# A fused attention and token/channel mixer: the short tile's weight parts stacked, the last pair's products in another order, and other orders for the planner

## The chip, the cores and the metric

The kernel runs on one core of a Trainium2 chip. The metric is the device time of one execution in microseconds. Matmuls run on TensorE (PE; its weight loads appear as PEld), elementwise work on VectorE (DVE), ScalarE (ACT) and GpSimd (POOL). SyncE (SP) issues the DMA transfers in this kernel; they leave its queue in order.

## The reference

For 8 batches of 8 heads, 576 positions and width 64, two attentions are added: one on q, k and v averaged over groups of four positions (144 x 144 scores, the result repeated four times), and a local one with scores for |i - j| < 4. The result x (576 x 512 per batch) goes through a token MLP across the positions and a channel MLP:

```python
q_d = q.reshape(B, H, Sd, 4, D).mean(axis=3)     # also k_d, v_d
out_up = np.repeat(sm_attn(q_d, k_d, v_d), 4, axis=2)
scores = np.where(np.abs(pos[:, None] - pos[None, :]) < 4, scale * q @ k.T, -1e9)
x = out_up + softmax(scores) @ v
h = np.maximum(x.T @ w_tok1, 0) @ w_tok2         # 576 -> 256 -> 576
u = x + h.T
out = u + np.maximum(u @ w_ch1, 0) @ w_ch2       # 512 -> 1536 -> 512
```

## The kernel before

**Attention.** Per batch, `pool_q` and `load_v` sum q, k and v in groups of four (qd, vd; v arrives in eight pieces, vr). `pooled` works on four pairs of heads: scores sd (line 503), their row maximum mxd, the exponential pd, its transpose td (line 531), the product ad with vd (line 541), and the division into od (line 551). `pd` is made in two ways: in the batches of `BIASED` ACT takes the exponential with the negative maximum as bias, four instructions a pair (line 515); in the others DVE subtracts (line 521, two a pair) and ACT takes one exponential (line 524). `local` works on five tiles of positions (`TILES`; four of 128 rows, the last, short one of 64): scores sc, the masked softmax P (line 600 multiplies by the reciprocal sum r), its transpose pT, copied to pt, and the product av with vw (line 619). vw holds v for the local windows in its rows, loaded with line 466, and in further rows the pooled result od, written there by a DMA (line 557): so one av product gives the sum of both attentions. av has to wait for that write.

**Token MLP** (`mix`). t1 adds up, over the five tiles, x of a tile times the first token weight. In batch 0 x and W are plain float32 (line 672). From batch 1 on both are split in a high part and the remainder (xh, made by ACT, line 658, and DVE, line 660; W1[t] has the two parts side by side), and `mm3` multiplies three of the four combinations (`PASSES`: high by high, high by remainder, remainder by high). In the short tile only 64 of the 128 partitions hold data. t2 is the second token product; its result plus x is scaled and split as uh, in 16 bit.

**Channel MLP.** Batches 0 and 1 are computed plainly (c1 from uh and CW, c2 from h and CX). Batches 2 to 7 use a seven-product scheme on 2 x 2 blocks: `first_blocks` goes over six pairs n, each with the products B11, T1, T2, B22, B21, T3 and T4, collected in cx, cy and cz, and in the loop T3 and T4 of a pair stand among the products of the next pair; `after` makes the sums s, y, u and the inputs h of the second layer from them (s reads cz, y reads cx after T3, and T4 may only be added to cx when y has read it). `second_blocks` then makes 2 x 7 products dX, dY, dZ of 18 matmuls each, that is 3 for each of the six pairs.

**Order.** No engine's order is written by hand. Every piece of work is a generator that says with `step(engine, us, needs...)` what it would run next; `drive` (lines 172 to 212) keeps a clock per engine and takes the step that can start first. Among steps on one engine that start within `PATIENCE` of each other it takes the one whose generator stands first in the list; `PRIORITY` is the order of the groups in that list (p pooled, A local, W and w token weights, U the up part of batch 0, and so on). While batch 0's uh is not ready, `keep_busy` fills gaps on PE with matmuls of a constant tile ("busy<-junk"). SP's order follows from the same steps; a weight load also waits until the third load before it has landed (`in_turn`). In SP's order C1 to C2 names the channel weights (raw), W0 to W8 the token weights (raw).

Of the kernel before, what the change touches and what calls it, by code (L numbers as in the profile page):

```python
# [6 lines left out]
F32 = mybir.dt.float32  # L7
F32R = mybir.dt.float32r
F16 = mybir.dt.float16
# [26 lines left out]
DEPTH = 3  # L36
PRIORITY = "LpWUMASETaCDPHmQw"


@with_exitstack  # L40
def tile_ups_attention_mixer(ctx, tc, qk, vw, vr, w1, w2, c1, c2, out):
# [83 lines left out]

    def mm3(ps, lhs, rhs, first, last, **kw):
        for i, (a, c) in enumerate(PASSES):
            nc.tensor.matmul(ps, lhs(a), rhs(c), start=first and i == 0, stop=last and i == 2, **kw)  # L128

# [10 lines left out]

    clock = dict(A=2.0, G=5.0, V=2.0, P=0.0, S=0.0, D=0.0, R=0.0, X=0.0)
    now = [0.0]
# [29 lines left out]
    def drive(streams):  # L172
# [3 lines left out]
        while True:  # L176
# [37 lines left out]
    def to_f32(raw, at, y=None, *needs):  # L214

        n = raw.shape[1] // 2
        words = raw.rearrange("p (n two) -> p n two", two=2)
        lo, hi = words[:, :, 0], words[:, :, 1]
        yield step("A", 0.1 + n * 0.0011, at=at)
        nc.scalar.activation(hi.bitcast(F32), hi.bitcast(F32), AF.Prelu, scale=2.0 ** -112, alpha=-2.0 ** 32)  # L220
        yield step("G", 0.1 + n * 0.0016)

        nc.gpsimd.tensor_scalar(lo, lo, 2.0 ** -29, -0.501, ALU.mult, ALU.add)
        e = yield step("V", 0.08 + n * 0.0012, *needs, port=True)
        nc.vector.scalar_tensor_tensor(lo if y is None else y(), hi, 3, lo, ALU.logical_shift_left, ALU.bitwise_or)
        return e
# [48 lines left out]
    class Channel:  # L275
# [31 lines left out]
        def parts(self, i):  # L307
            y = self.place[i + 2]
            f = self.place[i].bitcast(F16).rearrange("p (a n) -> p a n", a=2)
            yield step("A", 0.72)  # L310
            nc.scalar.activation(f[:, 0], y, AF.Copy, scale=self.s[i // 4])
            t = yield step("V", 0.75, port=True)
# [102 lines left out]
    def load_v(st):  # L415
# [53 lines left out]
    def pool_q(st, hp):  # L469
# [92 lines left out]
    def local(st, t):  # L562
# [35 lines left out]
        nc.vector.reciprocal(r, r)  # L598
        yield step("V", 0.5, at=0.0, port=True)
        nc.vector.tensor_tensor(w, w, r.unsqueeze(2).unsqueeze(2).to_broadcast([n, H, 8, 5]), ALU.mult)  # L600
        before = [("av", b, t - 2)] if t > 1 else [("av", b - 1, 3 + t)] if b else []
# [42 lines left out]
    def mix(st):  # L644
# [8 lines left out]
        def splits():  # L653
            for t in range(NT if b else 0):
                yield step("A", 0.62, ("x", b, t), *([("over", 0, 0)] if b == 1 else []),
                           *([("t1", b, t - 3)] if t > 2 else [("mixed", b - 1)] if b > 1 else []))
                xh = st.xh[t] = T([128, 2, 512], F32R, "xh", f"xh{b}_{t}")
                nc.scalar.copy(xh[:, 0], xf(t))
                e = yield step("V", 0.7, port=True)
                nc.vector.tensor_tensor(xh[:, 1], xf(t), xh[:, 0].bitcast(F32), ALU.subtract)  # L660
                make(("xh", b, t), e)

        def products():
            for t in range(NT):
                e = yield step("P", 1.8 if b == 0 else 1.5 if b == 1 else 1.42, *([("W", "split", t), ("xh", b, t)] if b else [("W", "y", t), ("x", 0, t)]),
                               take="" if t else f"gg>{b}")
                if t == 0:
                    st.acc = P2(f"t1_{b}")
                for f in range(2):
# [342 lines left out]

    PER_BATCH = 12 + 2 * len(SECOND)
    blocks_ = {}

    def first_blocks(b):
# [13 lines left out]

        for n in range(NP + 1):
            m = n - 1
            if n < NP:
                p = blocks_[b, n] = Batch()
                e = yield go(n, 0, "B11", take=f"m>X{b}_{n}")
                p.h = T([128, 7, 2, HALF], F16, "h7", f"h{b}_{n}")
                H.append(p.h)
                p.a = unit[base + 2 * n]
                p.X = PM(f"cx{b}_{n}")[:, :HALF]
                product(p.X, p.a[:, 0], "B11", True)  # L1040
                make(("product", b, n, "B11"), e)
            if m >= 0:
                q = blocks_[b, m]
                e = yield go(m, 1, "T3", ("uc", b, m))
                product(q.X, q.b[:, 1], "T3", False)
                make(("product", b, m, "T3"), e)
            if n < NP:
                e = yield go(n, 0, "T1", take=f"m>Y{b}_{n}")
                p.Y = PM(f"cy{b}_{n}")[:, :HALF]
                product(p.Y, p.a[:, 1], "T1", True)  # L1050
                make(("product", b, n, "T1"), e)
            if n < NP:
                e = yield go(n, 0, "T2", ("s", b, n))
                product(p.X, p.a[:, 2], "T2", False)
                make(("product", b, n, "T2"), e)
            if m >= 0:
                e = yield go(m, 1, "T4", ("c22", b, m))
                product(q.X, q.b[:, 2], "T4", False)
                make(("product", b, m, "T4"), e)
                make(("used", base + 2 * m + 1), e)  # L1060
            if n < NP:
                e = yield go(n, 0, "B22", ("y", b, n))
                product(p.Y, p.a[:, 3], "B22", False)
                make(("product", b, n, "B22"), e)
                make(("used", base + 2 * n), e)
                e = yield go(n, 1, "B21", take=f"g>Z{b}_{n}")
                p.b = unit[base + 2 * n + 1]
                p.Z = P1(f"cz{b}_{n}")[:, :HALF]
                product(p.Z, p.b[:, 0], "B21", True)
                make(("product", b, n, "B21"), e)  # L1070
        make(("first", b), e)

    def after(b, n):
# [82 lines left out]
        def z_chain():  # L1156
# [6 lines left out]
            make(("got", "t4", b, n), e)  # L1163
            e = yield step("V", 0.46, give=f"m>X{k}")
            lo_relu("B21", p.X)
# [11 lines left out]
    def second_blocks(b):  # L1177
# [3 lines left out]

        def product(ps, w, x, first_):
            i = PARTS.index(x)
            for k in range(6):
                for j, (a, c) in enumerate(PASSES):
                    nc.tensor.matmul(ps, w[:, k, a], H[k][:, i, c], start=first_ and k == j == 0,  # L1186
                                     stop=k == 5 and j == 2, skip_group_check=True)

        for o in range(2):
            at = st.at = {}  # L1190
            for i, name in enumerate(SECOND):
# [3 lines left out]
                needs = [] if new else [("into", b, o, {"S2": "A11", "S3": "S2", "A22": "S3", "S4": "S1"}[name])]  # L1195
                e = yield step("P", 2.21, ("unit", k), *(("h", b, n, OF[name]) for n in range(len(FIRSTS))), *needs,
                               at=0.0, take="" if not new else f"m>{kind}{b}_{o}z")
                if new:
                    at[kind] = PM(f"d{kind}{b}_{o}")[:, :HALF]
                product(at[kind], unit.pop(k), OF[name], new)  # L1200
                blocks_[b, o, name] = at[kind]
# [181 lines left out]
```

## Time and profile before

| | us |
|---|---|
| median of 3 runs | 897.86 |
| lowest, highest | 896.86, 899.55 |
| the profiled execution | 899.88 |
| its span, first to last instruction | 897.9 |
| PE, DVE, ACT, POOL busy | 857.5, 634.4, 418.9, 395.1 |

The span leaves out 2.0 us of the profiled execution's time, before the first and after the last instruction. Its mean granted clock is 0.974 of full speed. In the rows below a timeline row has start, duration, engine, line, operation, "out<-in", shapes and a count; in brackets stands the idle time before it, and what ended it. A group's row has busy time and mean duration behind the bar, then idle time and its releasers. A wait's row has total, number and longest.

### The profile page before, as it was taken

What the parts mean: (1) busy time and instruction counts of PE and PEld (TensorE: products, weight loads), DVE (VectorE), ACT (ScalarE), POOL (GpSimd) and SP (SyncE); (2) the same over time, 40 slices, a digit from 0 to 9 for tenths busy, and PEclk for the clock granted to TensorE, in tenths of its full rate; (3) what the DMA queues carried; (4) which work ended last, traced back from release to release, by engine and by line L of the source; (5) the groups of instructions that cost most, each with busy time, mean ns of one, the idle gap of its engine ahead of it and who ended that gap; (6) DMA issues with size and microseconds to landing.
All of it is one profiled execution on the core that took longest, in us unless ns stands there. A gap on an engine that the chain in (4) does not pass through costs nothing.

```text
span 897.9 us, 26687 instructions
## 1 busy us (share of the span) xinstructions
PE 857.5 (95%) x11112; PEld 691.5 (77%) x11112; DVE 634.4 (71%) x1410; ACT 418.9 (47%) x978; POOL 395.1 (44%) x593
## 2 busy tenths in 40 slices
PE   8798999898999999999999999999999999999998
PEld 6666777686779877888778887878768786887776
DVE  6669999667886756858576876678576875656662
ACT  2366553134553335744375526654265525642640
POOL 6228475868596203662077404752067401420330
PEclk9589999898999999999999999999999999999999
DMA  7875523663364308645673466544664464237653
GB/s 243 283 263 192 164 63 118 233 209 93 95 222 118 92 27 291 218 127 158 197 275 121 134 199 230 200 139 156 223 233 137 130 196 124 95 112 214 203 161 122
DMA packets 71656, 152.85 MB, mean 170 GB/s; under 512 B 16560, under 2 KB 32432, under 8 KB 69488
## 3 DMA queue, kind: packets, MB, share of 16 engines
q1 hardware_dynamic: 71536, 151.16, 51.5%
q8 instruction: 87, 1.43, 0.6%
q14 instruction: 33, 0.27, 0.1%
HBM read 128.32 MB, written 20.45 MB: 166 GB/s over the span
## 4 chain that ended last, share of the span: by engine, by line
PE 81%; DVE 9%; DMA 4%; ACT 2%; POOL 2%; issue 2%; SPq 1%; ACTq 0%; DVEq 0%; POOLq 0%
PE dX L1186 12%; PE c L128 11%; PE t L128 11%; PE cx L1025 10%; PE dY L1186 6%; PE cy L1025 6%; PE ad L541 3%; PE cz L1025 3%; PE dZ L1186 3%; PE av L619 3%; PE sc L577 2%; PE pT L605 2%; PE td L531 2%; PE sd L503 2%; PE t L690 2%
## 5 line engine op out<-in xcount | busy, mean ns | idle before, releaser
L1098 POOL TENSOR_TENSOR h<-t,h 128x288 f16<-128x288 f32 x108 | 83.2, 772 | 213.6 <-ACT h L1087 212.6
L1025 PEld LDWEIGHTS <-wa 128*128 128x128 f16 x864 | 82.3, 98 | 27.1 <-issue 4.7
L1186 PEld LDWEIGHTS <-wc_S 128*128 128x128 f16 x864 | 83.4, 98 | 21.0 <-issue 0.2
L1025 PEld LDWEIGHTS <-wb 128*128 128x128 f16 x648 | 63.0, 99 | 20.1 <-issue 3.9
L128 PE MATMUL c<-h,CX 128*128 128x288 f16 x576 | 76.3, 289 | 0.6 <-DVE CX L313 0.5
L128 PE MATMUL c<-uh,CW 128*128 128x288 f16 x576 | 75.2, 286 | 0.4 <-issue 0.4
L1186 PEld LDWEIGHTS <-wc_A 128*128 128x128 f16 x648 | 62.9, 98 | 15.7 <-issue 0.2
L487 POOL TENSOR_TENSOR qd<-qk 128x144 f32<-128x144 f32 x48 | 30.9, 644 | 87.5 <-DMA qk<-in_qk_dram 87.5
L128 PEld LDWEIGHTS <-CX 128*128 128x128 f16 x576 | 55.6, 99 | 16.4 <-DVE CX L313 1.2
L128 PEld LDWEIGHTS <-CW 128*128 128x128 f16 x576 | 55.1, 98 | 14.3 <-issue 1.0
L1025 PE MATMUL cx<-uh_T,wb 128*128 128x288 f16 x432 | 64.9, 287 | 1.1 <-DVE y L1129 1.1
L457 POOL TENSOR_TENSOR vr<-vr 72x256 f32<-72x256 f32 x48 | 37.0, 770 | 60.3 <-DMA vr<-in_vr_dram 51.2
L128 PE MATMUL t<-xh,W 128*128 128x512 f32 x210 | 58.8, 414 | 4.7 <-DVE xh L660 2.5
L487 POOL TENSOR_TENSOR qd<-qd,qk 128x144 f32<-128x144 f32 x96 | 60.6, 631 | 6.3
L128 PE MATMUL t<-W,hid 128*128 128x288 f32 x336 | 58.4, 309 | 0.0
L1186 PE MATMUL dX<-h,wc_S 128*128 128x288 f16 x432 | 56.9, 286 | 0.0
L1186 PE MATMUL dY<-h,wc_S 128*128 128x288 f16 x432 | 56.9, 286 | 0.0
L1186 PE MATMUL dX<-h,wc_A 128*128 128x288 f16 x432 | 56.0, 286 | 0.0
L1087 ACT ACTIVATE h<-t 128x288 f16<-128x288 f32 x108 | 47.6, 442 | 12.6 <-DVE t L1102 12.5
L1227 DVE SCALAR_TENSOR_TENSOR u<-dX,io,u 128x288 f32<-128x288 f32 x48 | 24.8, 517 | 34.0 <-PE dX L1186 33.7
L128 PEld LDWEIGHTS t<-xh,W 128*128 128x128 f32 x210 | 37.1, 188 | 15.2 <-DVE xh L660 5.1
L128 PEld LDWEIGHTS t<-W,hid 128*128 128x128 f32 x336 | 46.6, 189 | 0.0
(206 smaller groups left out, 1957.5 us busy)
## 6 DMA issues: line engine op xcount, KB each, us to landing
qk<-in_qk_dram SPq DMA_DIRECT2D x32, 580.0 KB
wa<-d1a SPq DMA_DIRECT2D x36, 512.0 KB
wc_S<-d_S SPq DMA_DIRECT2D x48, 384.0 KB
wb<-d1b SPq DMA_DIRECT2D x36, 384.0 KB
wc_A<-d_A SPq DMA_DIRECT2D x36, 384.0 KB
vw<-in_vw_dram SPq DMA_DIRECT2D x8, 1280.0 KB
vr<-in_vr_dram SPq DMA_DIRECT2D x64, 144.0 KB
vw<-in_vw_dram SPq DMA_DIRECT2D x8, 1024.0 KB
```

Source lines behind the costliest of these rows:

```text
L128: nc.tensor.matmul(ps, lhs(a), rhs(c), start=first and i == 0, stop=last and i == 2, **kw)
L457: nc.gpsimd.tensor_add(t[:, 0:2], t[:, 0:2], t[:, 2:4])
L487: nc.gpsimd.tensor_add(to, to if f > 1 else x[0], x[f])
L503: nc.tensor.matmul(ps[:G, par, Sd * g:Sd * g + Sd], st.qd[p, pr, 0, G * g:G * g + G], st.qd[p, pr, 1], start=True, stop=True)
L531: nc.tensor.transpose(ps[:G, par, o:o + G], pd[:, par, g, G * kg:G * kg + G], ident[:G, :G])
L541: nc.tensor.matmul(ps[:, g, par], pt[:, par, kg, G * g:G * g + G], st.vd[:, kg, 2 * pr + par], start=kg == 0, stop=kg == 1)
L619: nc.tensor.matmul(ps[QB * j:QB * j + QB, par, D * hp:D * hp + D], pt[p, hp, QB * j:QB * j + QB], st.vw[p, g, h, D * hp:D * hp + D], start ...
L1025: nc.tensor.matmul(ps, w[:, a, 128 * k:128 * k + 128], uh[x][:, k, c], start=first_ and k == j == 0, stop=k == 1 and j == 2, skip_group_ch ...
L1087: nc.scalar.activation(here().h[:, PARTS.index(name), 0], x, f)
L1098: nc.gpsimd.tensor_tensor(h[:, i, 1], getattr(here(), x), h[:, i, 0], ALU.subtract)
L1186: nc.tensor.matmul(ps, w[:, k, a], H[k][:, i, c], start=first_ and k == j == 0, stop=k == 5 and j == 2, skip_group_check=True)
L1227: nc.vector.scalar_tensor_tensor(u, blocks_[b, o, name], io, u, ALU.mult, ALU.add)
```

## The change

- The short tile's two weight parts are stacked: the high part in partitions 0 to 63 and the remainder in 64 to 127 of one half of W1, the high part once more in the other half. xh of the short tile has the high part of x in both halves of the partitions (two copies by ACT). Two passes (`STACKED`) then cover the three combinations.
- In `first_blocks` the last pair's T3 stands ahead of its B21, and T4 behind it. In `second_blocks` the products of o = 0 are divided: 15 matmuls for the first five pairs, then 3 for the last, which alone need the last pair's h.
- vr of batch 0 lies in the eight buffers of u instead of those of x, xh and od.
- `BIASED` holds all batches; P times r runs on POOL in batch 0; batch 7's cx lies in the "gg" banks.
- `PATIENCE`, `PRIORITY`, the costs of several steps and the filler's size (at most 12 instead of 8, for 0.85 instead of 0.6 of a gap) are other numbers.

```diff
+STACKED = ((0, 0), (1, 1))
-PATIENCE = 0.15
+PATIENCE = 0.1
-BIASED = range(2, 8)
+BIASED = range(0, 8)
-PRIORITY = "LpWUMASETaCDPHmQw"
+PRIORITY = "pLSUMAWTaCEDPHmQw"
...
-                    keep_busy(min(8, int((t - clock["P"]) * 0.6 / 0.22)))
+                    keep_busy(min(12, int((t - clock["P"]) * 0.85 / 0.22)))
...
         nc.scalar.copy(f[:, 0], WY[i])
+        if f.shape[0] == short:
+            nc.scalar.copy(f[:, 1], WY[i])
...
-        nc.vector.tensor_tensor(f[:, 1], WY[i], f[:, 0].bitcast(F32), ALU.subtract)
+        nc.vector.tensor_tensor(W1[-1][short:, 0] if f.shape[0] == short else f[:, 1], WY[i], f[:, 0].bitcast(F32), ALU.subtract)
...
-            tag = "x" if st.b or i < 4 else "xh" if i < 7 else "od"
-            ts[i] = T([G, 4, 128], F32, tag, f"vr{st.b}_{i}")
+            ts[i] = T([G, 4, 128], F32, "x" if st.b else "u", f"vr{st.b}_{i}")
...
-        nc.vector.tensor_tensor(w, w, r.unsqueeze(2).unsqueeze(2).to_broadcast([n, H, 8, 5]), ALU.mult)
+        (nc.gpsimd if b < 1 else nc.vector).tensor_tensor(w, w, r.unsqueeze(2).unsqueeze(2).to_broadcast([n, H, 8, 5]), ALU.mult)
...
-                nc.scalar.copy(xh[:, 0], xf(t))
+                if t < NT - 1:
+                    nc.scalar.copy(xh[:, 0], xf(t))
+                else:
+                    for p in (0, short):
+                        nc.scalar.copy(xh[p:p + short, 0], xf(t)[:short])
...
-                            t == 0, t == NT - 1)
+                            t == 0, t == NT - 1, PASSES if t < NT - 1 else STACKED)
...
+            if n == NP - 1:
+                yield from third(n)
+            e = yield go(n, 1, "B21", take=f"g>Z{b}_{n}")
+            p.b = unit[base + 2 * n + 1]
+            p.Z = P1(f"cz{b}_{n}")[:, :HALF]
+            product(p.Z, p.b[:, 0], "B21", True)
+            make(("product", b, n, "B21"), e)
+        e = yield from fourth(NP - 1)
...
+                early = NP - 1 if o == 0 else NP
...
+                product(at[kind], w, OF[name], new, range(early))
+                if early < NP:
+                    e = yield step("P", 2.21 / NP, ("h", b, early, OF[name]), at=0.0)
+                    product(at[kind], w, OF[name], False, range(early, NP))
```

Three places show how the orders differ. The first is SP's queue in the opening, where od0's write to vw0 is issued. Before:

```order
L241 DMA C15_raw_495<-in_c1_dram 128x1024
L241 DMA W5_raw_602<-in_w2_dram 128x576
L241 DMA W6_raw_627<-in_w2_dram 128x576
L241 DMA W7_raw_692<-in_w2_dram 128x576
L241 DMA W8_raw_706<-in_w2_dram 128x576
L557 DMA vw0_338<-od0_452 8x9x512 x2
L241 DMA C16_raw_892<-in_c1_dram 128x1024
```

and now:

```order
L242 DMA C15_raw_589<-in_c1_dram 128x1024
L242 DMA W5_raw_775<-in_w2_dram 128x576
L559 DMA vw0_412<-od0_425 8x9x512 x2
L242 DMA W6_raw_793<-in_w2_dram 128x576
L242 DMA W7_raw_799<-in_w2_dram 128x576
L242 DMA W8_raw_871<-in_w2_dram 128x576
L242 DMA C16_raw_915<-in_c1_dram 128x1024
```

The write has moved past the loads of W6, W7 and W8.

The second is PE's order where batch 2's pooled attention begins (the first number in a name is the batch, the second of sd, td and ad the pair of heads; c1_1_0_0 is a plain product of batch 1). Before:

```order
L503 MATMUL sd2_0_3158<-qd2_2411 72x144 x4
L503 MATMUL sd2_1_3169<-qd2_2411 72x144 x4
L531 MATMUL td2_0_3190<-ident_67,pd2_0_3179 72x72 x8
L531 MATMUL td2_1_3209<-ident_67,pd2_1_3200 72x72 x8
L541 MATMUL ad2_0_3233<-vd2_2819,ptd2_0_3221 72x65 x8
```

and now, where sd2_0 and sd2_1 stand directly ahead of c1_1_0_0's twelve matmuls, of which the first row is the last:

```order
L129 MATMUL c1_1_0_0_3265<-uh1_0_3_3241,CW0_140 128x288
L637 MATMUL um1_1_t_3290<-ident_67,um1_1_m_3281 1x128
L533 MATMUL td2_0_3293<-ident_67,pd2_0_3257 72x72 x8
L643 MATMUL um1_1_b_3305<-um1_1_m1_3292,ones_72 128x1
L533 MATMUL td2_1_3312<-ident_67,pd2_1_3283 72x72 x8
L129 LDWEIGHTS CW1_141
```

A whole product of batch 1 has come in between sd and td, and ad2_0 has moved behind a further one.

The third is DVE's order at the end of batch 7's last pair (number 5), before:

```order
L1091 SCALAR_TENSOR_TENSOR h7_4_13135<-cx7_4_13136,h7_4_13135 128x288
L1111 TENSOR_TENSOR s7_5_13234<-cz7_5_13279,s7_5_13234 128x288
L1151 TENSOR_TENSOR u7_5_13264<-cy7_5_13238,u7_5_13264 128x288
L1129 TENSOR_TENSOR y7_5_13253<-cx7_5_13217,y7_5_13253 128x288
L1102 SCALAR_TENSOR_TENSOR t17_5_13315<-s7_5_13234,u7_5_13264 128x288
```

and now:

```order
L1168 TENSOR_TENSOR u7_5_13336<-cy7_5_13310,u7_5_13336 128x288
L1108 SCALAR_TENSOR_TENSOR h7_4_13209<-cx7_4_13210,h7_4_13209 128x288
L1128 TENSOR_TENSOR s7_5_13306<-cz7_5_13364,s7_5_13306 128x288
L1146 TENSOR_TENSOR y7_5_13327<-cx7_5_13291,y7_5_13327 128x288
L1119 SCALAR_TENSOR_TENSOR t17_5_13387<-s7_5_13306,u7_5_13336 128x288
```

u has moved ahead of s; y stands behind s in both, while on PE the product that s reads (B21) now comes after the one that y reads (T3).

Over the program the order has 9702 rows on PE instead of 9574; among them 216 junk matmuls instead of 152 and 196 products t<-xh,W instead of 210.

More of the change, by code (lines that the diff above doesn't have):

```diff
@@ L124, in tile_ups_attention_mixer, with mm3 @@
         nc.vector.tensor_copy(p[:, :, 3:53:7], rep.unsqueeze(1).to_broadcast([128, H, QB // 4]))
-    def mm3(ps, lhs, rhs, first, last, **kw):
-        for i, (a, c) in enumerate(PASSES):
-            nc.tensor.matmul(ps, lhs(a), rhs(c), start=first and i == 0, stop=last and i == 2, **kw)
+    def mm3(ps, lhs, rhs, first, last, passes=PASSES, **kw):
+        for i, (a, c) in enumerate(passes):
+            nc.tensor.matmul(ps, lhs(a), rhs(c), start=first and i == 0, stop=last and i == len(passes) - 1, **kw)
     def pow2(src, f, inv, s, least=2.0 ** -60):
@@ L134, in pow2 @@
         nc.vector.reciprocal(s, inv)
[L141 removed]
+    clock = dict(A=2.0, G=5.0, V=2.0, P=0.0, S=0.0, D=1.5, R=0.0, X=0.0)
     now = [0.0]
@@ L1013, in tile_ups_attention_mixer, with X_IN @@
     PER_BATCH = 12 + 2 * len(SECOND)
+    def X_IN(b):
+        return "gg" if b == B - 1 else "m"
     blocks_ = {}
@@ L1029, in go @@
             return step("P", 0.74, ("unit", base + 2 * n + u), ("uh", b, x), *needs, at=0.0, take=take)
[L1031 to L1070, printed above, removed]
@@ new lines, in third, with fourth @@
+        def third(m):
+            q = blocks_[b, m]
+            q.b = unit[base + 2 * m + 1]
+            e = yield go(m, 1, "T3", ("uc", b, m))
+            product(q.X, q.b[:, 1], "T3", False)
+            make(("product", b, m, "T3"), e)
+        def fourth(m):
+            q = blocks_[b, m]
+            e = yield go(m, 1, "T4", ("c22", b, m))
+            product(q.X, q.b[:, 2], "T4", False)
+            make(("product", b, m, "T4"), e)
+            make(("used", base + 2 * m + 1), e)
+            return e
@@ new lines, in first_blocks @@
+        for n in range(NP):
+            p = blocks_[b, n] = Batch()
+            e = yield go(n, 0, "B11", take=f"{X_IN(b)}>X{b}_{n}")
+            p.h = T([128, 7, 2, HALF], F16, "h7", f"h{b}_{n}")
+            H.append(p.h)
+            p.a = unit[base + 2 * n]
+            p.X = (PM(f"cx{b}_{n}") if X_IN(b) == "m" else P2(f"cx{b}_{n}")[:, 0])[:, :HALF]
+            product(p.X, p.a[:, 0], "B11", True)
+            make(("product", b, n, "B11"), e)
+            if n:
+                yield from third(n - 1)
+            e = yield go(n, 0, "T1", take=f"m>Y{b}_{n}")
+            p.Y = PM(f"cy{b}_{n}")[:, :HALF]
+            product(p.Y, p.a[:, 1], "T1", True)
+            make(("product", b, n, "T1"), e)
+            e = yield go(n, 0, "T2", ("s", b, n))
+            product(p.X, p.a[:, 2], "T2", False)
+            make(("product", b, n, "T2"), e)
+            if n:
+                yield from fourth(n - 1)
+            e = yield go(n, 0, "B22", ("y", b, n))
+            product(p.Y, p.a[:, 3], "B22", False)
+            make(("product", b, n, "B22"), e)
+            make(("used", base + 2 * n), e)
+            if n == NP - 1:
[5 more added lines that the diff above has]
+            make(("product", b, n, "B21"), e)
@@ L1180, in second_blocks, with product @@
         H, base = st.H, PER_BATCH * (b - 2) + 12
-        def product(ps, w, x, first_):
+        def product(ps, w, x, first_, ks):
             i = PARTS.index(x)
-            for k in range(6):
+            for k in ks:
                 for j, (a, c) in enumerate(PASSES):
@@ L1195, in second_blocks @@
                 needs = [] if new else [("into", b, o, {"S2": "A11", "S3": "S2", "A22": "S3", "S4": "S1"}[name])]
-                e = yield step("P", 2.21, ("unit", k), *(("h", b, n, OF[name]) for n in range(len(FIRSTS))), *needs,
+                NP = len(FIRSTS)
+                early = NP - 1 if o == 0 else NP
+                e = yield step("P", 2.21 * early / NP, ("unit", k), *(("h", b, n, OF[name]) for n in range(early)), *needs,
                                at=0.0, take="" if not new else f"m>{kind}{b}_{o}z")
```

20 lines of the change are left out of this document (10 added, 10 removed).

## The prediction

> **What bounds the kernel now.** I read the page first, then the list of waits by engine, then windows by stage, then the timeline of the places that stood out.
>
> ```profile
> span 897.9 us, 26687 instructions
> PE 857.5 (95%) x11112; PEld 691.5 (77%) x11112; DVE 634.4 (71%) x1410; ACT 418.9 (47%) x978; POOL 395.1 (44%) x593
> ```
>
> TensorE is busy 857.5 of 897.9 us, the next engine 71% of them: TensorE is the bound. There are three ways to gain: fewer matmuls, fewer of the 40.4 idle us, and fewer matmuls at a low clock. The windows (PE busy, then the other engines, then PEclk in the third column from the right) say where idle and low clock lie:
>
> ```profile
> 0.00:85.00 85.00, 72.92 (x1034) 56.71 (x1035) 60.59 (x142) 41.27 (x82) 41.18 (x78) 0.84 0.70 239
> 131.00:250.00 119.00, 107.59 (x1653) 87.50 (x1652) 89.89 (x197) 46.02 (x101) 78.83 (x112) 0.94 0.46 151
> 345.00:898.00 553.00, 538.32 (x6645) 435.14 (x6633) 377.08 (x843) 270.12 (x661) 205.89 (x307) 1.00 0.54 174
> ```
>
> The first 85 us lose 12.1 us to idling and run at 0.84, 131 to 250 lose 11.4 at 0.94, the long rest from 345 on loses 14.7 out of 553. So the opening and the stage of batch 1 hold most of what an order of work can win. PE's waits over the run:
>
> ```profile
> PE av L619 <- DMA vw<-od: 7.6, 5, 3.1
> PE td L531 <- ACT pd L515: 7.5, 5, 3.2
> PE t L128 <- DVE xh L660: 2.5, 3, 1.8
> PE t L128 <- ACT xh L658: 2.0, 2, 1.2
> ```
>
> **A: the write of od0 leaves SP earlier.** SP's timeline and the chain of waits:
>
> ```profile
> 20.07 12.45 SPq L241 DMA_DIRECT2D C_raw<-in_c_dram  x6
> 33.56 5.58 SPq L241 DMA_DIRECT2D W_raw<-in_w_dram  x4
> 39.19 1.56 SPq L557 DMA_DIRECT2D vw<-od  x2
> 40.06 4.16 DMA vw<-od
> 35.41 0.42 DVE L551 TENSOR_TENSOR od<-ad,rd 72x256 f32<-72x256 f32 x1
> 46.23 5.48 PE L672 MATMUL t<-x,W_y 128*128 128x512 f32 x8
> 55.33 3.70 PE L672 MATMUL t<-x,W_y 128*128 128x512 f32 x8
> ```
>
> od0 is finished at 35.83, but its write stands behind four W loads, issued from 33.56 to 39.14. It is issued at 39.19, lands at 44.22, and the av matmuls wait for it. Afterwards it stands behind the first W load only, at about 33.9. For that od0 must be done by then: before, the od buffer waited for POOL's last read of vr0_7; now v lies in other buffers and the pd subtractions are off DVE. With the same 5.0 us from issue to landing, av starts 39.2 - 33.9 = 5.3 us earlier. The eight t matmuls after it cost 5.48 us against 3.70 warm: another 1.8 if the shorter idling keeps the clock. If od0 were no earlier than 35.83, the write could go then: -3.4. The far end is 0, if the loads under way hold its landing where it is. I take **-5.3**, since both issue times are in rows. The POOL multiply by r replaces one on DVE ahead of pT; POOL waited for loads in these microseconds, so I cost it at nothing; if it queues behind a conversion there, the price is about that of DVE's part of one, 0.62 in the rows below.
>
> **B: the first c products.** Per group on DVE or PE:
>
> ```profile
> L521 DVE TENSOR_TENSOR pd<-sd,mxd 72x288 f32<-72x288 f32 x16 | 6.5, 448 | 0.3
> L600 DVE TENSOR_TENSOR P<-P,r 128x320 f32<-128x320 f32 (+1 forms) x40 | 21.2, 530 | 0.7
> L510 DVE TENSOR_SCALAR mxd<-mxd 72x4 f32<-72x4 f32 x24 | 6.4, 267 | 0.8
> L515 ACT ACTIVATE pd<-sd,mxd 72x144 f32<-72x144 f32 x96 | 28.3, 373 | 26.2 <-DVE mxd L510 14.2 <-PE ad L541 10.9 <-issue 1.1
> L524 ACT ACTIVATE pd<-pd 72x576 f32<-72x576 f32 x8 | 5.5, 682 | 19.7 <-DVE pd L521 19.6
> 47.72 2.48 DVE L225 SCALAR_TENSOR_TENSOR CW<-C_raw 128x512 uint32<-128x512 uint32 x4
> 72.07 1.14 DVE L225 SCALAR_TENSOR_TENSOR CW<-C_raw 128x512 uint32<-128x512 uint32 x1
> 82.33 2.04 PE L170 MATMUL busy<-junk 128*128 128x192 bf16 x13
> 84.54 1.65 PE L128 MATMUL c<-uh,CW 128*128 128x288 f16 x12
> 92.88 8.98 PE L128 MATMUL c<-uh,CW 128*128 128x288 f16 x72
> ```
>
> Ahead of the first c's input DVE loses 8 pd (8 x 0.448 = 3.6) and 5 products by r (5 x 0.53 = 2.7), and gains 5 CW conversions (5 x 0.62 = 3.1) and 4 mxd multiplies (4 x 0.267 = 1.1): net 2.1 less. On PE, 13 junk matmuls (2.04) fill the time until c, and from 84.54 to 92.88 four groups of 1.65 take 8.34 us, a loss of 1.7. So 3.7 can go at most, nothing at least. I take **-2.1**, DVE's saving, because DVE holds that stretch. The five conversions then no longer sit between c products. The softmax of a pair in batches 0 and 1 was a chain of two pd on DVE and one exp on ACT, 2 x 0.448 + 0.682 = 1.58; now it is four exps on ACT, 4 x 0.373 = 1.49. On the path that is even; ACT works 0.81 more per pair, 3.2 per batch, which its idle half (41.27 of 85 us busy) covers; uncovered it would eat the 2.1.
>
> A price that speaks against this part: one CW conversion took 0.62 us with POOL idle (first of the two CW rows) and 1.14 at 72 us, with POOL at work. The Trainium skill, SBUF — State Buffer, "Who interferes with whom", says that a VectorE instruction with two SBUF inputs contends with a GpSimd instruction that reads SBUF; these two rows agree. By that rule the five multiplies now on POOL could each lengthen a conversion by 0.5, 2.6 in all, and B would come out at +0.5.
>
> **C: batch 1's start, 131 to 250.**
>
> ```profile
> 168.42 1.46 SPq L557 DMA_DIRECT2D vw<-od  x2
> 171.81 0.27 PE L619 MATMUL av<-vw,pt 64*32 64x64 f32 x2 [2.44 <-DMA vw<-od]
> 176.06 3.08 PE L128 MATMUL c<-h,CX 128*128 128x288 f16 x12
> 212.64 0.69 PE L531 MATMUL td<-ident,pd 72*72 72x72 f32 x8 [3.21 <-ACT pd L515]
> 214.14 1.18 PE L531 MATMUL td<-ident,pd 72*72 72x72 f32 x8 [0.80 <-ACT pd L515]
> 215.00:220.00 5.00, 5.00 (x156) 4.41 (x154) 2.96 (x9) 0.98 (x3) 4.47 (x9) 0.50 0.21 57
> ```
>
> Before, td of batch 2 stood right behind sd and waited 3.21 + 0.80 = 4.0 us; now c products of batch 1, independent of the softmax, stand between: -4.0, nothing late behind them but td itself, which has 12 products (1.65 us) and more of cover. The clock was 0.50 behind this gap, and low behind the 2.4 us wait for vw1 too: the c row at 176 takes 3.08, where the same twelve took 1.65 at 84.54. Half clock cost about 1.5 there and 2.5 behind td (half of the five us from 215). I take 2.0 of these 4.0, the share of the td gap, and leave the 3.7 us of av waits in this window as they are. Bounds: 0, if new waits take their place, and -15 (11.4 idle plus 4 of clock). I take **-6.0**.
>
> The Trainium skill, TensorE: Matmul & The Clock Gate, "Part 1: The HAM clock gate", has the array fall to half rate after an idle window of about 3.4 us and return after as much busy time. The 3.21 gap with 0.50 behind it agrees nearly; a 2.44 gap was enough at 171.81, so the measured one decides. By the rule alone the 216 junk matmuls (152 before) would keep the opening warm too, and A would be -7.1.
>
> **D: batches 2 to 7.** The waits there are those of 345 to 898, and the end of batch 7's last pair:
>
> ```profile
> PE td L531 <- ACT pd L515: 3.5, 3, 1.2
> 861.91 0.45 DVE L1129 TENSOR_TENSOR y<-cx,y 128x288 f32<-128x288 f32 x1
> 862.42 0.90 PE L1025 MATMUL cx<-uh_T,wb 128*128 128x288 f16 x6 [0.55 <-DVE y L1129]
> ```
>
> In batches 2 to 5 the first 15 matmuls of a second step now run between sd and td: they hide the 3.5. In batches 6 and 7 nothing is left to put there, and T4 waits for y as before. But y stands behind s on DVE, and s reads B21's sum, which PE now computes after T3. B21 ends where T3 did, 861.87 by the row of T4 less its wait; s and y, of 0.45 each, then end near 862.8: T4 is 0.4 later, twice, +0.8 (0 if DVE catches up). Together **-2.7**, bounds +0.8 and -5.7 (the xh waits of 2.5 and 2.0 gone as well, the tail at nothing).
>
> **E: the short tile.**
>
> ```profile
> 258.98 1.39 PE t L128 x6
> L128 PE MATMUL t<-xh,W 128*128 128x512 f32 x210 | 58.8, 414 | 4.7 <-DVE xh L660 2.5 <-ACT xh L658 2.0
> L658 ACT CAST xh<-x_last 128x512 fp32r<-128x512 f32 x7 | 4.3, 610 | 0.1
> ```
>
> Two passes instead of three take away 7 x 2 = 14 matmuls. They issue every 1.39 / 6 = 0.23 us (the mean of 414 ns holds the overlap): -3.3. Seven casts become fourteen of half the partitions; by this row, at equal length per row, 0.61 more on ACT per batch. If each delayed its t it would be +4.3; PE waited for such a cast twice in seven batches, and usually has other batches' products, so I add one, 0.6: **-2.7**.
>
> The rest (batch 7's X in another bank, the filler's size) is cost at nothing: banks show no wait in the rows, and junk fills gaps; a misjudged gap costs a run like that at 82.33, 2.0.
>
> **Sum**: -5.3 - 2.1 - 6.0 - 2.7 - 2.7 = -18.8. The profiled execution took 899.88 us (span plus 2.0), 2.0 above the median of the runs; 899.9 - 18.8 - 2.0 = **879**.
>
> **Rivals.**
> 1. The middle gives nothing: td's 4.0 comes back as another wait, because ACT and DVE lag at the same places (DVE is busy 76% of 131 to 250). Then 879 + 6 = 885. For it: the order changes nothing in ACT's work. Against: products stand there now.
> 2. The opening gives nothing, bound by its loads: C and W loads fill 20 to 39 us, and all of C must land before c. A and B vanish: 879 + 7.4 = 886. With 1 as well: 892. That is also the case in which the change does not do what it says: the write leaves SP earlier and av still waits.
> 3. Everything holds in full: A -7.1, B -3.7, C -10, D -4, E -3.3: -28, or 870.
> 4. Slower. vw1's write stands on SP now behind an output store of u0 and a store of S2 that waits for POOL. Such waits were long:
>
> ```profile
> SPq L892 <- DVE u L891: 36.0, 8, 17.0
> SPq L912 <- POOL S L955: 23.0, 6, 7.5
> ```
>
> If the store waits the full 17.0 past the time at which od1 is ready, av1 and all of PE behind it stand still. C turns from -6 to about +17: 879 + 23 = 902. It decides slower only from about 16 us of lateness; before, the write came at 168.42, after such stores too.
>
> **How the numbers follow.** The likeliest, all terms near the taken values (873 to 884): 0.50. Rival 1 or 2 alone (884 to 889): 0.19; both (889 to 895): 0.06. Rival 3 (864 to 873): 0.12. Nearly no change (895.2 to 900.6, terms A, B and C gone and a new wait as well): 0.05. Rival 4: 0.08. The range of 866 to 893 leaves out rival 4, no change and the ends of 3 and of "both": 0.2. A measurement of this kernel can tell about 0.3%, 2.7 us, from no change. Faster: 0.87; same 0.05; slower 0.08.
>
> **What the profile would show.** A: the vw<-od issue near 34 on SP, av near 39, clock above 0.84 in the first 80 us. B: the first c near 77 and no gap of over 1 us behind it. C: no td wait of 3 us near 205, and PEclk 1.00 behind it. D: dX matmuls between sd and td, T4 of batches 6 and 7 still waiting for y, by about 1 us. E: t<-xh,W x196. Wrong if PE idles as long elsewhere: above all for vw<-od, xh or um.

## The result, and the profile after

| | before | after |
|---|---|---|
| median, us | 896.86 (7 runs) | 903.31 (7 runs) |
| lowest to highest | 891.7 to 899.55 | 899.36 to 906.08 |
| the profiled execution | 899.88 | 906.08 |

The ratio after to before is 1.0072, 95% interval 1.0043 to 1.0101: the change made the kernel slower by 0.7%, where 2% faster was forecast. Both profiled executions lie about 3 us above their medians. Of the fourteenth and the sixteenth run below, one execution each took 1210 and 1390 us at a granted clock of 0.65 and 0.56; the ratios leave such executions out.

The head of the page after:

```profile
span 904.0 us, 26801 instructions
PE 852.4 (94%) x11162; PEld 688.3 (76%) x11162; DVE 622.6 (69%) x1396; ACT 428.1 (47%) x1010; POOL 400.3 (44%) x599
```

PE has 5.1 us less work, and yet the span is 6.1 longer: its idle time rose from 40.4 to 51.6. To see where, the run is cut at the first cx matmul, that is at batch 2's first block. The windows up to it and from it, of before and then of after (columns as in the prediction):

```profile
0.00:336.55 336.55, 310.75 (x4295) 249.59 (x4296) 252.98 (x558) 143.72 (x306) 189.19 (x286) 0.94 0.49 161
336.55:897.90 561.35, 546.77 (x6819) 441.95 (x6816) 381.46 (x852) 275.18 (x672) 205.89 (x307) 1.00 0.54 176
```

```profile
0.00:345.38 345.38, 311.26 (x4355) 250.73 (x4356) 243.49 (x544) 148.02 (x333) 194.09 (x292) 0.94 0.48 157
345.38:904.00 558.62, 541.14 (x6809) 437.56 (x6806) 379.13 (x852) 280.05 (x677) 206.25 (x307) 1.00 0.55 177
```

The part up to the cut, from which 13.4 us less were forecast (A, B, C), takes 8.8 more. The rest (D, E: 5.4 less) takes 2.7 less. PE's waits after:

```profile
PE av L621 <- DMA vw<-od: 12.2, 5, 7.7
PE cy L1035 <- ACT y L1143: 7.2, 4, 1.9
PE c L129 <- DVE uh L770: 5.3, 3, 2.6
PE sc L579 <- issue: 4.3, 3, 2.8
PE cx L1035 <- DVE h L1108: 3.0, 4, 0.9
PE td L533 <- ACT pd L517: 1.3, 1, 1.3
```

The td waits of 7.5 shrank to 1.3, as forecast. But three waits stand there that before did not have (cy for y, c for uh, cx for h), the wait of av for vw is longer, and in sc PE stands still for 4.3 us (before 0.4) for nothing that the trace shows ("issue"). These are the places.

**The opening.** PE from the gap in sc on, the DVE and SP rows around od0's write, and PE's two waits for it:

```profile
25.76 0.47 PE L579 MATMUL sc<-qk 64*32 64x40 f32 x20 [2.84 <-issue]
26.17 3.06 PE L171 MATMUL busy<-junk 128*128 128x192 bf16 x18
35.97 0.63 DVE L226 SCALAR_TENSOR_TENSOR W_y<-W_raw 128x256 uint32<-128x256 uint32 x1
37.96 0.42 DVE L553 TENSOR_TENSOR od<-ad,rd 72x256 f32<-72x256 f32 x1
36.67 0.33 SPq L242 DMA_DIRECT2D W_raw<-in_w_dram  x1
38.41 1.53 SPq L559 DMA_DIRECT2D vw<-od  x2
41.45 0.27 PE L621 MATMUL av<-vw,pt 64*32 64x64 f32 x2 [1.91 <-DMA vw<-od]
43.55 2.04 PE L621 MATMUL av<-vw,pt 64*32 64x64 f32 x126 [1.84 <-DMA vw<-od]
```

The write is one load behind C15 instead of four. But od0 is done at 38.38 instead of 35.83, and the write follows it at once: it leaves 0.8 us earlier, not 5.3. W5, the load ahead of it, had left at 36.67 (before 33.56), when the conversion of W0 (W_y), whose buffer it takes, was done. Behind both lies the gap of 2.84 us and what follows it: 18 junk matmuls run in 3.06 us, and only then, at 29.02, comes the td whose exponentials had been ready since 24.93. The granted clock from 20 to 34 us is 0.76.

That lies in this execution, and not in the order alone. The fourth run below changes only where batch 7's cx lies, and up to 843 us all its engines have the same order, so its trace shows this opening a second time:

```profile
22.20 0.33 PE L579 MATMUL sc<-qk 64*32 64x40 f32 x20 [1.17 <-issue]
22.46 1.66 PE L171 MATMUL busy<-junk 128*128 128x192 bf16 x18
33.51 0.33 SPq L242 DMA_DIRECT2D W_raw<-in_w_dram  x1
33.93 1.54 SPq L559 DMA_DIRECT2D vw<-od  x2
39.59 2.04 PE L621 MATMUL av<-vw,pt 64*32 64x64 f32 x126 [0.91 <-DMA vw<-od]
```

There the gap is 1.17 us, the clock from 20 to 34 is 1.00, and the write leaves at 33.93, where the prediction had it. The second and the third run, with the same order up to here, have the long gap again (writes at 37.77 and 37.97). Why the gap differs is not known.

**The first c products.** DVE and PE from 81 us on:

```profile
81.77 0.50 DVE L770 SCALAR_TENSOR_TENSOR uh<-u,us,uh 128x288 f16<-128x288 f32 x1
82.19 2.24 DVE L316 SCALAR_TENSOR_TENSOR CW<-CW,C_s,CW 128x512 f16<-128x512 f32 x2
84.35 0.92 DVE L770 SCALAR_TENSOR_TENSOR uh<-u,us,uh 128x288 f16<-128x288 f32 x1
85.19 1.95 DVE L316 SCALAR_TENSOR_TENSOR CW<-CW,C_s,CW 128x512 f16<-128x512 f32 x2
87.07 1.40 DVE L770 SCALAR_TENSOR_TENSOR uh<-u,us,uh 128x288 f16<-128x288 f32 x1
88.39 2.01 DVE L316 SCALAR_TENSOR_TENSOR CW<-CW,C_s,CW 128x512 f16<-128x512 f32 x2
90.33 0.92 DVE L770 SCALAR_TENSOR_TENSOR uh<-u,us,uh 128x288 f16<-128x288 f32 x1
...
88.52 0.53 PE L129 MATMUL c<-uh,CW 128*128 128x288 f16 x3 [2.58 <-DVE uh L770]
91.30 0.64 PE L129 MATMUL c<-uh,CW 128*128 128x288 f16 x2 [2.25 <-DVE uh L770]
93.18 3.09 PE L129 MATMUL c<-uh,CW 128*128 128x288 f16 x12
```

Between the four pieces of uh that the first c product needs stand six divisions of C1's tiles by their scale (CW<-CW,C_s,CW); before there was one. The first c starts when it did (84.16; before 84.54), waits three times for uh, and then runs cold (3.09 us for twelve matmuls). The 48th c matmul starts at 99.7 us; before it was at 92.5. From there to the first cx the delay only grows from 7.2 to 8.8. In the fourth run's trace, with its quicker opening, the 48th c still comes 3.5 us later than before (96.0) and the first cx 6.4 later (342.9).

**Batch 1's av.** DVE's od1, SP's issue, the chain, PE, and SP's waits from 161.2 to 172 us:

```profile
160.77 0.42 DVE L553 TENSOR_TENSOR od<-ad,rd 72x256 f32<-72x256 f32 x1
170.58 2.08 SPq L559 DMA_DIRECT2D vw<-od  x2
161.12 10.84 DMA qk<-in_qk_dram
171.98 5.20 DMA vw<-od
176.59 0.39 PE L621 MATMUL av<-vw,pt 64*32 64x64 f32 x2 [7.69 <-DMA vw<-od]
SPq L457 <- DMA vw<-in_vw_dram: 2.2, 1, 2.2
SPq L898 <- DMA vw<-in_vw_dram: 2.1, 1, 2.1
SPq L559 <- DMA qk<-in_qk_dram: 1.7, 2, 1.0
SPq L918 <- DMA qk<-in_qk_dram: 1.0, 1, 1.0
SPq L898 <- DVE u L897: 0.3, 1, 0.3
```

od1 is ready at 161.19, and its write is issued 9.4 us later. Before it was 9.4 us too (159.02 to 168.42). But before, batch 2's qk was loaded ahead of vw1 (from 151.90 and 156.12), and the last thing to land was vw1's load. Now the qk loads stand between that load and the write (from 159.90). SP waits 4.3 us for the load of vw1 and then 2.7 for those of qk, 0.7 of it between the write's two halves, and only 0.3 for u. In the chain the write follows a load of that qk and takes 5.20 us; before it took 3.18. PE is there no later than before, although it is 7 us behind at the 48th c: 444 c matmuls stand ahead of this av instead of 504.

**Batches 2 to 7.** One of the four cy waits, and in batch 7 the pair that repeats:

```profile
562.77 0.90 PE L1035 MATMUL cy<-uh_B,wa 128*128 128x288 f16 x6 [1.93 <-ACT y L1143]
854.40 0.46 DVE L1128 TENSOR_TENSOR s<-cz,s 128x288 f32<-128x288 f32 x1 [0.51 <-PE cz L1035]
854.77 0.45 DVE L1108 SCALAR_TENSOR_TENSOR h<-cx,h 128x288 f16<-128x288 f32 x1
855.27 0.90 PE L1035 MATMUL cx<-uh_B,wa 128*128 128x288 f16 x6 [0.91 <-DVE h L1108]
868.44 0.90 PE L1035 MATMUL cx<-uh_T,wb 128*128 128x288 f16 x6 [0.91 <-DVE y L1146]
```

h<-cx is the last read of cx's bank; it stands behind s<-cz on DVE and so waits for B21's end, and the next B11 waits for it. Before, h stood ahead of s. The last row is the T4 wait that the prediction had: 0.91, forecast about 1.

### The profile page after: what moved, and what is told of

The parts are those of the page before. It is cut to its first block, busy times and chain, and to the rows that moved or that the text cites. A ratio compares the mean times of both kernels' runs of the same rounds, so it can differ in the third digit from the quotient of the medians.

```text
span 904.0 us, 26801 instructions
## 1 busy us (share of the span) xinstructions
PE 852.4 (94%) x11162; PEld 688.3 (76%) x11162; DVE 622.6 (69%) x1396; ACT 428.1 (47%) x1010; POOL 400.3 (44%) x599
## 3 DMA queue, kind: packets, MB, share of 16 engines
q1 hardware_dynamic: 71536, 151.16, 51.6%
## 4 chain that ended last, share of the span: by engine, by line
PE 83%; DVE 9%; DMA 3%; ACT 3%; issue 2%; POOL 0%; SPq 0%; ACTq 0%; DVEq 0%
PE c L129 12%; PE dX L1203 12%; PE t L129 11%; PE cx L1035 10%; PE dY L1203 6%; PE cy L1035 5%; PE ad L543 3%; PE av L621 3%; PE dZ L1203 3%; PE cz L1035 3%; PE sc L579 2%; PE sd L505 2%; PE pT L607 2%; PE busy L171 2%; PE td L533 2%
## 5 line engine op out<-in xcount | busy, mean ns | idle before, releaser
L129 PE MATMUL c<-uh,CW 128*128 128x288 f16 x576 | 78.4, 290 | 5.4 <-DVE uh L770 5.3
L489 POOL TENSOR_TENSOR qd<-qk 128x144 f32<-128x144 f32 x48 | 28.0, 582 | 93.4 <-DMA qk<-in_qk_dram 90.0
L129 PE MATMUL t<-xh,W 128*128 128x512 f32 x196 | 55.4, 415 | 1.6 <-ACT xh L661 1.2
L517 ACT ACTIVATE pd<-sd,mxd 72x144 f32<-72x144 f32 x128 | 37.7, 373 | 26.3 <-DVE mxd L512 15.5
L666 DVE TENSOR_TENSOR xh<-x,xh 128x512 fp32r<-128x512 f32 x28 | 21.0, 749 | 40.9 <-ACT xh L661 40.9
```

The source lines that it names most:

```text
L489: nc.gpsimd.tensor_add(to, to if f > 1 else x[0], x[f])
L517: nc.scalar.activation(pd[:, par, g], s[:, par, g], AF.Exp, bias=mx[:, par, g:g + 1], scale=0.125 / 16)
```

## The experiments

Ratios are to the kernel before on the same chip, with their 95% intervals; the changed kernel's is 1.0072. The runs went to several chips, so differences in us between them are worked out from the ratios (0.1% is 0.9 us). Times of single places, such as the first cx, come from one execution each; the two traces of one order (345.4 and 342.9) show how far these can differ.

**All structural parts, old numbers.** The changed kernel with the planner's numbers of before.

```diff
-PATIENCE = 0.1
+PATIENCE = 0.15
-PRIORITY = "pLSUMAWTaCEDPHmQw"
+PRIORITY = "LpWUMASETaCDPHmQw"
...
-clock = dict(A=2.0, G=5.0, V=2.0, P=0.0, S=0.0, D=1.5, R=0.0, X=0.0)
+clock = dict(A=2.0, G=5.0, V=2.0, P=0.0, S=0.0, D=0.0, R=0.0, X=0.0)
-                    keep_busy(min(12, int((t - clock["P"]) * 0.85 / 0.22)))
+                    keep_busy(min(8, int((t - clock["P"]) * 0.6 / 0.22)))
...
```

> The changed kernel with the planner's old numbers (PRIORITY, PATIENCE, step costs, clock, filler); every other part of the change stays. Theory N (the new numbers lose the time, the structural parts gain): the short tile's 14 fewer matmuls give -3 and the td waits -3 against the kernel before, the two new waits at the end of batches 2 to 7 take some of it back, so about 4 us faster than before (ratio 0.995), and no wait of c for uh. Rival S (the structural parts load ACT, DVE and POOL so that they lose it themselves): as slow as the changed kernel, ratio 1.007.

Measured 894.99, ratio 0.9975 (0.995 to 1.0). No wait of c for uh. So the parts are worth about 2 us, with an interval that ends at nothing, and the numbers turned that into a loss of 6.5.

**The divisions held back.**

```diff
-                yield step("A", 0.0, ("C1", "scale", i // 4))
+                yield step("A", 0.0, ("C1", "scale", i // 4), *([("uh", 0, 0)] if i > 3 else []))
```

> The changed kernel, with the division of C1's tiles 4 to 11 (CW by C_s on DVE) held back until batch 0's first uh is done. Theory D (eight of these divisions stand between the four uh pieces on DVE; PE waits 5.3 us for uh and then runs cold): 5 to 7 us less than the changed kernel, ratio to before about 1.000, first c products without a wait for uh. Rival: DVE is simply full there, the divisions are missed later and c waits for CW instead: ratio stays at 1.007.

Measured 897.63, ratio 1.0021 (0.9992 to 1.0051). PE's rows at the same place:

```profile
84.40 1.63 PE L129 MATMUL c<-uh,CW 128*128 128x288 f16 x12
...
87.04 1.63 PE L129 MATMUL c<-uh,CW 128*128 128x288 f16 x12 [0.44 <-DVE C_mx L301]
...
88.91 4.58 PE L129 MATMUL c<-uh,CW 128*128 128x288 f16 x36
```

No wait for uh and none for CW: the 48th c starts at 91.7 instead of 99.7, the first cx at 335.75 instead of 345.38. By the ratios the run is 4.6 us faster than the changed kernel. Theory D holds: DVE had room, it was the place of the divisions (six among the uh pieces by the trace, not eight).

**Batch 2's qk behind the write to vw1.**

```diff
-        yield step("S", 0.1, *(("sc", b - 1, t) for t in every))
+        yield step("S", 0.1, *(("sc", b - 1, t) for t in every), *([("full", 1)] if b == 2 else []))
```

> The changed kernel, with the load of batch 2's qk (and vr) held back until batch 1's od has been issued to vw1. Theory W (the write of vw1 stands behind the loads of qk2 in the DMA queues and PE waits 7.7 us for it): the wait falls to 2 to 3 us and the time by about 5, ratio 1.002. Rival: the wait moves on, sd of batch 2 waits for its later qk: ratio 1.007.

Measured 898.6, ratio 1.0019 (0.9989 to 1.005). The write goes out at 166.70, and batch 1's first av starts at 169.61 instead of 176.59, with no wait over 1.5 us; sd of batch 2 comes at 212.8 instead of 220.09. SP still waits 3.6 us for u in between, but the write now goes out when the load of vw1 has landed, and takes 3.27 us. By the ratios the run is 4.8 us faster than the changed kernel. Theory W holds for this place: batch 2's loads held both the issue and the landing.

**Batch 7's cx in the m banks.**

```diff
-        return "gg" if b == B - 1 else "m"
+        return "m"
```

> The changed kernel, with batch 7's cx in the m banks as before. Theory X (with two gg banks instead of three m banks each B11 of batch 7 waits 0.9 us for the last read of the pair before): the waits cx<-h of 3.0 us go, 3 us less than the changed kernel, ratio 1.004. Rival: the three m banks are then short for cy, and the same microseconds appear there: ratio 1.007.

Measured 905.44, ratio 1.0101 (1.0047 to 1.0156): no gain. The waits cx<-h are still there, three of 0.91 us (the changed kernel had a fourth of 0.25). Theory X fell: the third bank does not help when the read that frees it stands behind s on DVE.

**PATIENCE 0.15 again, alone.**

> The changed kernel with PATIENCE 0.15 as before; nothing else. On ACT y<-cy stands ahead of h<-t again, and on DVE of batch 7 h<-cx ahead of s<-cz; five divisions still stand among the uh pieces. Theory P (PATIENCE made the waits of batches 2 to 7): cy<-ACT y falls from 7.2 to about 3.5 and cx<-h from 3.0 to 0, 6 to 7 us less than the changed kernel, ratio 1.000; the wait of c for uh stays. Rival: these waits come from T3's new place, they stay, ratio 1.007.

Measured 893.25, ratio 0.9975 (0.9949 to 1.0002). The two waits fell as expected, cy<-ACT y to 3.5 and cx<-DVE h to 0.4. But the time, 8.7 us less by the ratios, came from elsewhere: the first cx is at 332.46 instead of 345.38, and the stretch from there on is 559.84, no shorter than the 558.62 of the changed kernel. Other waits grew there, cx for y from 0.9 to 2.6 and t for xh from 1.6 to 3.3. The reading of P was right in its rows and wrong in its sum.

**The old PRIORITY, alone.**

> The changed kernel with the old PRIORITY string; PATIENCE and the costs stay new. Two divisions instead of six stand among the uh pieces, and the write of od0 stands behind W8 again. Theory D (the string's late E group put the divisions there): the wait of c for uh falls from 5.3 to about 1, and 5 us less than the changed kernel, ratio 1.002. Rival R (what is gained there is lost by the later write of od0, as the string was meant to win it): within 1 us of the changed kernel, ratio 1.007.

Measured 894.5, ratio 0.9986 (0.9962 to 1.0011): 7.7 us less than the changed kernel by the ratios, more than expected. The 48th c comes at 92.0, c waits 0.9 us for uh, and the first cx comes at 333.91.

**Both repairs.** The held divisions and PATIENCE 0.15.

> Both in one: the divisions of tiles 4 to 11 held until batch 0's first uh is done, and PATIENCE 0.15. If D and P are two separate losses, their gains add: 6 (r2) + 6 to 7 = 12 less than the changed kernel, ratio 0.993. If they are one loss seen at two places, no more than 7: ratio 0.999.

Measured 891.68, ratio 0.9948 (0.9915 to 0.998): 11 us less than the changed kernel by the ratios, and the interval holds the 0.993 of two separate losses and not the 0.999 of one. But the fifth run, with PATIENCE alone, had 893.25 on the same chip, and the spread of either is larger than the 1.6 us between them: that the held divisions gain on top of PATIENCE 0.15 is not shown.

**The new numbers on the old structure.** The kernel before, with the new PRIORITY, PATIENCE, step costs, clock and filler.

> The other way round: the kernel before, with the new numbers alone (PRIORITY, PATIENCE, step costs, clock, filler) and none of the structural parts. Theory N (the numbers lose it): slower than before by 7 to 10 us, ratio 1.009; the order has three divisions among the uh pieces and h<-cx behind s<-cz in four pairs of batch 7. Rival (the numbers are good by themselves, and only fit the new structure badly): ratio below 1.000.

Measured 907.6, ratio 1.0129 (1.0098 to 1.0161). Its first cx is at 335.64, 0.9 earlier than before; the stretch from there on is 570.36 instead of 561.35. So with the old structure the same numbers lose at another place.

**The stacked short tile alone**, with its step costs.

```diff
...
-                yield step("A", 0.62, ("x", b, t), *([("over", 0, 0)] if b == 1 else []),
+                yield step("A", 0.62 if t < NT - 1 else 1.2, ("x", b, t), *([("over", 0, 0)] if b == 1 else []),
...
-                            t == 0, t == NT - 1)
+                            t == 0, t == NT - 1, PASSES if t < NT - 1 else STACKED)
```

> The kernel before with the stacked short tile alone; the planner's numbers and its order around it stay. Theory (term E): 14 matmuls of 0.23 us fewer, less one late cast, 2.7 us, ratio 0.997, t<-xh,W x196. Rival: the second copy on ACT makes the short tile late and its wait takes the gain: ratio 1.000.

Measured 898.71, ratio 1.0013 (0.9987 to 1.004). The t group is 3.0 us shorter (55.8 for 196 against 58.8 for 210), and cy waits 3.5 us for ACT's y in four batches.

**The new blocks alone** (`first_blocks` and `second_blocks` of the change).

> The kernel before with the last pair's T3 ahead of its B21 and the divided second steps alone. Theory (term D): the td waits of 3.5 us go, the end of batches 6 and 7 costs 0.8, ratio 0.997. Rival: B22 of a later pair waits for y instead (0.9 us in four batches, as in the runs with the old numbers), and nothing is left: ratio 1.000 or above.

Measured 894.96, ratio 0.9967 (0.9937 to 0.9997). The td waits behind the first cx are gone, and cy does not wait for y there.

**The other structural parts alone** (v in the buffers of u, BIASED, P times r on POOL).

> The kernel before with the remaining structural parts alone: v of batch 0 in the buffers of u, BIASED for all batches, P times r of batch 0 on POOL; old numbers, old blocks, no stacking. Theory: the first run (all structural parts, old numbers) came to its first cx 3.8 us earlier than before, and these parts made it: ratio 0.997. Rival: they add work to ACT (3.2 us a batch) and POOL and lose, and stacking and blocks alone made that run's gain: ratio 1.002.

Measured 894.69, ratio 0.9982 (0.9956 to 1.0008): between the two, unclear.

**Three repairs.** The seventh run's kernel and the late qk of batch 2.

> All three repairs in the changed kernel: divisions held until batch 0's first uh, PATIENCE 0.15, batch 2's qk loaded behind the write to vw1. If the third is a loss of its own: 3 to 4 us less than the seventh run (0.9948), so 0.991, with no wait of av for vw above 3 us at batch 1. If PE only arrives earlier at the next wait: 0.995.

Measured 892.61, ratio 0.9971 (0.9938 to 1.0003): no gain over the seventh run. At batch 1 av waits 0.7 us for vw, as the edit meant; but in the seventh run the longest there was 1.4 already, against 7.69 in the changed kernel. In that order batch 2's qk was loaded ahead of vw1 (from 150.25 and 152.34), as before (2.44) and in the sixth run (0.7); in the fifth, with qk behind vw1, it was 7.3. So there was little left to win. The 5.3 us that are left as the longest wait for vw are batch 0's.

**PATIENCE 0.1 alone on the kernel before.**

```diff
-PATIENCE = 0.15
+PATIENCE = 0.1
```

> The kernel before with PATIENCE 0.1 alone. Theory P: the short patience by itself makes the waits of batches 2 to 7 (cy for ACT's y in four batches, cx for h<-cx behind s<-cz in batch 7); the stretch from the first cx on, 561.4 us before, becomes 567 to 570, as in the eighth run, ratio 1.008. Rival: PATIENCE hurts only with the new costs; ratio 1.000.

Measured 911.99, ratio 1.02 (1.0162 to 1.0237). The windows up to the first cx and from it:

```profile
0.00:345.60 345.60, 317.28 (x4301) 252.25 (x4302) 248.13 (x557) 143.31 (x306) 190.59 (x287) 0.92 0.49 157
345.60:913.30 567.70, 544.76 (x6819) 439.87 (x6816) 379.24 (x852) 277.95 (x672) 207.56 (x307) 1.00 0.54 174
```

The later stretch grew by 6.4, with the waits that the changed kernel has too: cy<-ACT y 7.3, cx<-DVE h 2.7. The earlier one grew by 9.0, with other waits than the changed kernel's; the 48th c is on time there (90.7). From 100 to 180 us PE idles 11.6 us instead of 7.0, at a clock of 0.89 instead of 0.96, and the longest wait is batch 1's av for vw, 4.56.

**The new PRIORITY alone on the kernel before.**

> The kernel before with the new PRIORITY alone. Five divisions stand among the uh pieces and the write of od0 two places ahead of W8. Theory D: c waits for uh as in the changed kernel, the 48th c product comes at 96 to 100 us instead of 92.5, ratio 1.005, and batches 2 to 7 are as before (561). Rival: the divisions only matter when ACT and POOL carry the extra work; ratio 1.000 or below.

Measured 901.16, ratio 1.0075 (1.0046 to 1.0103). PE at the first c:

```profile
84.17 0.62 PE L128 MATMUL c<-uh,CW 128*128 128x288 f16 x3 [2.10 <-DVE uh L764]
87.43 0.64 PE L128 MATMUL c<-uh,CW 128*128 128x288 f16 x2 [2.64 <-DVE uh L764]
```

These are the changed kernel's waits, with none of the structural parts: the string alone puts the divisions among the uh pieces. The 48th c starts at 97.9, the later stretch takes 559.08.

**The stacked short tile in the old order**, with the step costs left as they were, so that no engine's order changes but for the tile itself.

> The stacked short tile alone, with the planner's step costs left as before, so that every engine keeps its order of before. Theory: the 14 matmuls are worth their 3 us, and in the ninth run the new step costs moved other work and gave them back as 0.9 us waits of cy for y: ratio 0.997, no wait of cy for y. Rival: PE simply arrives 0.5 us earlier at the same y: ratio 1.000, with these waits.

Measured 894.0, ratio 0.9986 (0.9965 to 1.0007); the ninth run had 1.0013. cy does not wait for y, and the stretch from the first cx is 557.46 (561.35 before). The rival's waits are not there; the interval holds both 0.997 and 1.000, so the gain is seen in the trace, not in the time.

**A version from these runs**: the changed kernel with the divisions held, PATIENCE 0.15, cx in the m banks and the old step costs for the short tile.

> A version from what the runs showed: the changed kernel with the divisions held, PATIENCE 0.15, cx in the m banks and the old step costs for the short tile. If the seventh run's 0.9948 and the fifteenth run's gain add: 0.993. If the short tile's step costs do not matter: 0.995.

Measured 890.82, ratio 0.995 (0.9926 to 0.9974): faster than the kernel before and the changed one, and level with the seventh run. Its window up to the first cx:

```profile
0.00:329.76 329.76, 304.17 (x4362) 244.84 (x4363) 246.89 (x545) 147.66 (x333) 192.19 (x291) 0.99 0.51 164
```

The clock up to the first cx is 0.99 instead of 0.94. From there on cy does not wait for y and cx not for h.

## Why the prediction was wrong, by its own steps

**What it rested on.** Every term asked which wait of before would go. The planner's numbers had no term of their own; their effect was taken to lie in the orders that the terms used. The runs show the numbers as the largest part of the change: alone they cost 1.3%, PATIENCE alone 2.0%, PRIORITY alone 0.75%, while all structural parts without them gain 0.25% with an interval that ends at 1.0. These do not add up: each sets an order, and the orders lose at different places. Putting back either one of the two was worth 8 to 9 us in the changed kernel.

**A, forecast -5.3, was -0.7 in the profiled execution** (av's main group from 44.26 to 43.55) **and -4.7 in the fourth run's** (39.59). The issue order did what was forecast. The step that failed in the profiled execution is that od0 would be done by 33.9; it was 38.38, behind a gap of 2.84 us on PE and 18 junk matmuls at a low clock. The filler's size had been put at nothing. That the same order gave 33.93 once and 37.8 to 38.4 three times makes the size of A partly luck. The prediction's list of waits also leaves out one of this opening that the change took away, sd for DVE's pd, one of 3.1 us.

**B, forecast -2.1, was about +8** (the 48th c is 7.2 later in spite of A's 0.7; in the fourth run's trace 3.5 later in spite of 4.7). The step that failed is the count: the five instructions that DVE gains ahead of the first c's input were taken for conversions of raw tiles at 0.62 us. They are divisions by the scale, 0.75 to 1.1 us each, and, above all, they were summed as work anywhere in the stretch. Six stand among the four pieces of uh, where each of them delays PE. The second run shows it, and the fourteenth that the string did it. The price of 2.6 worked out with the rule of the Trainium skill, SBUF — State Buffer, "Who interferes with whom", was too small, but the rule names what is seen: with POOL busy (8.40 of the 9.20 us from 82.0) a uh instruction, two inputs in SBUF, took 0.92 to 1.40 us instead of 0.50. It is the smaller part: before, the four uh pieces took 3.1 us in all, now 3.7.

**C, forecast -6.0, was about +1.6** (from the 48th c to the first cx; +2.9 in the fourth run's trace). The td waits of this stretch went and the clock behind them is 1.00, as forecast. What failed is leaving the av waits as they were: the one at batch 1 is 7.69 instead of 2.44. Rival 4 had this place, but not its reason: between od1 and its write SP waited 0.3 us for u, and the 9.4 us to the issue were there before as well. What it left out is the load of batch 2's qk, ahead of the write at the issue and in the transfers, and the 60 c matmuls that PE now runs behind this av instead of ahead of it. The third run shows the part of the load.

**D and E, forecast -5.4 together, were -2.7.** D's mechanism held: the td waits behind the first cx are gone in the changed kernel and in the tenth run, and T4 waits 0.91, once. What the sum lacked are two waits in their place, 7.2 us of cy for y and 3.0 of cx for h. PATIENCE 0.1 alone makes both on the old structure (thirteenth run), and in the changed kernel they fall to 3.5 and under 1 with either number put back (fifth and sixth run). The 3.5 of cy that are left come with the short tile's step costs (3.5 in the ninth run, none in the fifteenth and sixteenth). The orders of ACT and DVE that make them were there to be read; only the last pair's was. E's matmuls were sized right: the t group fell from 58.8 to 55.4 us. The rival "the gain comes back as another wait" was given for the middle alone; it held for batches 2 to 7.

**The range** ended at 893 because the slower case was given 0.08. That five terms rest on one order, and that one misread row in it touches several of them, was not priced.

**What stays open.** Why the gap in sc is 1.17 us in one execution of the opening and 2.84 in another is not known. The 9 us that PATIENCE 0.1 costs up to the first cx on the old structure were not repaired one by one. And either number put back alone wins most of what both repairs win: which waits the changed kernel's 6.5 us are is shown by places, not as a sum.

## What to carry to other kernels

When numbers of a scheduler change, read the new order at every place where the bottleneck engine waits for another engine's short work, not only at the waits of before: here the largest loss came from six moved DVE instructions, visible in the order. Time such numbers and the structural parts apart; the parts alone came out 0.25% faster, at the edge of the noise, and a clearly faster version (0.5%) came from taking PATIENCE and a step cost back and holding one group of steps by an explicit need. Read a place from more than one trace before you blame the order for it. Where a small write feeds the bottleneck, see which loads stand ahead of it in the issuing queue and among the transfers.

## What the runs showed of the hardware

With POOL at work a DVE scalar_tensor_tensor of 128x288 with its inputs in SBUF took up to 1.40 us, where the same took 0.50 at another moment; a pair of 128x512 divisions took 1.95 to 2.24 us. Two gaps in PE's work before 91.3 us, of 2.58 and 2.25 with three matmuls between them, were enough for twelve matmuls at 93 us to take 3.09 us instead of 1.63; the granted clock was 0.92 from 82 to 91.2 and 0.50 from there to 95. One order had a granted clock of 0.76 from 20 to 34 us in one execution, behind a gap of 2.84, and 1.00 in another, behind 1.17. And a write of od behind the load of qk took 5.20 us; with that load held back it took 3.27, and before 3.18.
